# Turning the second item's queries by DMA behind a hold on the loads, with a reordered start, in a sorted-attention and maxout kernel

## The chip, the cores and the metric

The kernel runs on one core of a Trainium2 chip. The metric is the device time of one execution in microseconds. Thirteen executions of the kernel before gave a median of 167.15 us (166.62 to 169.05). A profile is one further execution taken apart by the hardware profiler; all times in it count from the start of its span.

The engines are TensorE (PE; the loading of its weights is listed as PEld), VectorE (DVE), ScalarE (ACT), GpSimd (POOL) and SyncE (SP). SP only issues DMAs here; GpSimd issues the loads[...].

## What is computed

Four items (batch entries) with 8 heads of 768 tokens and head dimension 64. The tokens of a head form 8 blocks of 96. A small matrix per head, made nearly doubly stochastic by five rounds of normalisation, mixes the blocks of keys and values ("sorts" them); attention then runs within each block, and a maxout layer with an output product follows on the 3072 tokens.

```python
for _ in range(5):
    P = P - np.max(P, axis=-1, keepdims=True)
    P = np.exp(P)
    P = P / (np.sum(P, axis=-1, keepdims=True) + 1e-09)
    P = P / (np.sum(P, axis=-2, keepdims=True) + 1e-09)
k_sorted = np.einsum('bhij,bhjcd->bhicd', P, k_b).reshape(B, H, S, D)
v_sorted = np.einsum('bhij,bhjcd->bhicd', P, v_b).reshape(B, H, S, D)
...
scores = scale * np.matmul(q_b, k_sb.transpose(0, 1, 2, 4, 3))
attn = softmax(scores)
out = np.matmul(attn, v_sb).reshape(B, H, S, D)
...
h1 = x @ w1
h2 = x @ w2
g = np.maximum(h1, h2)
return (g @ w_out).astype(np.float32)
```

Inputs and output are float32; the kernel computes in bf16 with float32 accumulation.

## The kernel before

The whole program is one unrolled list of steps, written by hand; every engine runs its share in that order. A pool `psum` of four tiles of 128 x 1024 float32 serves every product: a step that wants a tile waits until an earlier user has been read out. `evac` reads a tile out on ScalarE ("A") or VectorE ("D"); where the list doesn't say which, `pick` takes the one with the smaller account in `load`.

*Start.* The five normalisation rounds (`sinkhorn`, L271 to L290) are a chain of short VectorE instructions with one exponential per round on ScalarE. Meanwhile TensorE multiplies zeros: 86 matmuls of 142 columns at L764, and 3072 columns each in the fourth and fifth round, with zero weights (`late`) that are written when the round begins. VectorE also makes masks in the first three rounds (`masks`) and, in the third, the selections of item 0 (`selections(0, nc.vector)`). `turn_v` reorders item 0's values for the sort, mostly on ScalarE. `block_diagonals_first` turns the mixing matrix into the two operands of item 0's sorts.

*Front.* The string `front` at L779 is item 0 up to its maxout layer: `k` sorts a third of the keys, `v` a quarter of the values, `tq` turns half of the queries on TensorE, `SC` is a score step (products and one exponential), `VA` a value step (products, a reciprocal and a multiplication), `tx` transposes attention outputs, `tw` transposes one weight matrix, `h..a` and `h..b` are the two halves of a maxout product, `diff` subtracts the weight matrices on VectorE, `pe` makes the sort operands of items 1 to 3, and `F` puts 512 columns of zeros before the next score, value or maxout step. The first key sort has 1024 columns of zeros ahead of it.

*Tails.* From then on there is a list of units for each item: 8 maxout products (none left for item 0), for item 0 four products of the two output weights (`w_product`), and 12 output parts (`moe_out`; two of them fill half a tile, four are read out together). The dictionaries `first_tail`, `second_tail` and `third_tail` hang steps of the following items behind the unit of that number: `KS` (key sorts), `VS` (value sorts), `TQ` (query transposes), `SC`, `VA`, `TR` (attention outputs turned by DMA, issued by SP), `TURN` (a quarter of the value reordering, on VectorE). The value sort `sort_v_pair` handles items 1 and 2 together and needs all four turns; turns 1 and 2 read the first half of each item's values, turns 3 and 4 the second half.

*Queries.* `q_transposes` (L424) turns the queries so that head dimensions lie on partitions. Items 0 and 1 go through TensorE: 48 matmuls of 128 columns each item, and two evictions. Items 2 and 3 go through `pair_q` (two VectorE copies into `q_pair`) and two DMA transposes issued by SP.

*Loads.* All loads stand on GpSimd's queue, in the order of the program: values, keys and queries of item 0, the weights (w1 and w2 in quarters and a half, then the output weights), keys of item 1, queries of item 1, the values of items 1 and 2 in two pieces each, keys of item 2, queries of item 2 (into the space of w2), values of item 3 in four pieces (into the space of items 1 and 2, once these are turned), keys and queries of item 3. An issue that needs a buffer not yet free waits, and everything behind it on GpSimd waits too. GpSimd also writes the selections for the later items, `one_j`, and two weight differences.

## Time and profile before

| | us |
|---|---|
| median of 13 executions | 167.15 |
| the profiled execution | 166.62 |
| its span | 164.8 |
| TensorE busy | 159.4 |
| VectorE, ScalarE, GpSimd busy | 76.6, 83.0, 32.2 |
| first key sort starts | 12.14 |
| item 1's key sort starts | 37.98 |
| first value sort of items 1 and 2 starts | 50.83 |
| item 1's first maxout product starts | 70.59 |
| item 2's queries: first transpose issued, last landed | 73.00, 80.18 |
| item 3's last piece of values landed | 62.17 |

The groups of the page show the shape of the work: TensorE spends most of its time on two kinds of matmul.

```profile
L715 PE MATMUL out_ps<-wo_sb,g 128*128 128x512 bf16 (+2 forms) x200 | 48.3, 371 | 0.1
L688 PE MATMUL h_ps<-xT,w_sb 128*128 128x384 bf16 x256 | 44.5, 326 | 0.0
```

A row names the line, engine, operation and tiles, then the count; behind the first bar stand busy time in us and the mean length of one in ns, behind the second the idle time of the engine just before them. Matmuls overlap, so the mean length is not the distance between two of them: a matmul of 512 columns starts about 0.22 us after the one before it.

The page's sliced rows divide the span into 40 parts of 4.12 us; a digit is the busy share in tenths. The chain of waits is followed back from the last instruction to whatever released each step, and says what the end of the kernel hangs on. Timelines of one engine give start and length of each group of instructions.

### The profile page before, as it was taken

How to read it: one execution, taken by the hardware profiler on the slowest of the kernel's cores; microseconds unless marked ns; L12 is line 12 of the kernel's file. 1: busy time of each engine (PE TensorE's matmuls, PEld its weight loads, DVE VectorE, ACT ScalarE, POOL GpSimd, SP SyncE). 2: the span in 40 equal slices, each digit the busy share in tenths (PEclk: the TensorE clock that was granted, in tenths of full speed). 3: DMA queues.
4: the chain of work that ended last, by engine and by line, in shares of the span. 5: the costliest groups of instructions: out<-in, count | busy, mean ns of one | idle time of the engine just before them, and what ended most of it. 6: DMA issues, size and time to landing. Idle time of an engine off the chain costs nothing.

```text
span 164.8 us, 4562 instructions
## 1 busy us (share of the span) xinstructions
PE 159.4 (97%) x2018; PEld 96.1 (58%) x2018; DVE 76.6 (46%) x173; ACT 83.0 (50%) x102; POOL 32.2 (20%) x55
## 2 busy tenths in 40 slices
PE   7999899999999999999999999999999999999992
PEld 7948678656555555557555554575655546654451
DVE  5879789465474564625356973250642320000011
ACT  3585985927149846065653163557447206642020
POOL 7998396240113000000005020000000000000000
PEclk9999999999999999999999999999999999999999
DMA  3999999999999995689304999993025294000333
GB/s 46 205 204 198 198 207 206 211 203 223 211 201 211 216 241 95 183 107 241 68 0 77 154 218 199 265 224 21 0 52 175 50 164 142 0 0 0 127 131 127
DMA packets 30404, 23.90 MB, mean 145 GB/s; under 512 B 16752, under 2 KB 25200, under 8 KB 30384
## 3 DMA queue, kind: packets, MB, share of 16 engines
q0 software_dynamic: 11040, 13.37, 47.9%
q1 hardware_dynamic: 19200, 10.17, 27.5%
q8 instruction: 16, 0.26, 0.6%
q10 hardware_dynamic: 144, 0.07, 0.1%
q14 instruction: 4, 0.03, 0.1%
HBM read 26.75 MB, written 6.29 MB: 200 GB/s over the span
## 4 chain that ended last, share of the span: by engine, by line
PE 83%; DVE 9%; issue 3%; ACT 2%; DMA 1%; ACTq 0%
PE out_ps L715 34%; PE h_ps L688 26%; PE o_ps L586 4%; PE wc_ps L668 4%; PE s_ps L559 4%; PE k_ps L469 3%; PE tq_ps L444 2%; ACT e L567 2%; DVE v_dc L257 1%; PE v_ps L534 1%; PE tw_ps L649 1%; PE v_ps L490 1%; DMA p_sb<-in_sort_net_dram 1%; PE tx_ps L624 1%; DVE colsum L283 1%
## 5 line engine op out<-in xcount | busy, mean ns | idle before, releaser
L715 PE MATMUL out_ps<-wo_sb,g 128*128 128x512 bf16 (+2 forms) x200 | 48.3, 371 | 0.1
L688 PE MATMUL h_ps<-xT,w_sb 128*128 128x384 bf16 x256 | 44.5, 326 | 0.0
L688 PEld LDWEIGHTS <-w_sb 128*128 128x128 bf16 x256 | 24.0, 98 | 15.6
L567 ACT ACTIVATE e<-s_ps 96x768 bf16<-96x768 f32 x32 | 23.8, 805 | 13.5 <-PE s_ps L559 13.3
L702 ACT ACTIVATE g<-h_ps 128x768 bf16<-128x768 f32 x27 | 21.8, 810 | 17.5 <-PE h_ps L688 17.4
L715 PEld LDWEIGHTS <-g 128*128 128x128 bf16 x200 | 17.1, 97 | 15.8
L715 PE MATMUL out_ps<-wc,xT 128*128 128x512 bf16 (+2 forms) x100 | 24.8, 370 | 0.0
L108 ACT COPY o<-out_ps 128x1024 f32<-128x1024 f32 x10 | 10.1, 1012 | 28.3 <-PE out_ps L715 25.6
L603 DVE TENSOR_TENSOR x<-o_ps,rs 96x512 bf16<-96x512 f32 x32 | 22.0, 686 | 1.1
L715 PEld LDWEIGHTS <-xT 128*128 128x128 bf16 x100 | 9.6, 97 | 11.2
L586 PEld LDWEIGHTS <-e 96*128 96x128 bf16 x256 | 11.8, 97 | 5.9 <-DVE v_sb L110 0.2
L597 DVE RECIPROCAL rs<-o_ps 96x8 f32<-96x8 f32 x32 | 6.4, 201 | 17.8 <-PE o_ps L586 17.7
L750 DVE COPY o<-out_ps 128x512 f32<-128x512 f32 (+1 forms) x2 | 1.2, 625 | 27.6 <-PE out_ps L715 27.6
L586 PE MATMUL o_ps<-v_sb,e 96*128 96x65 bf16 x256 | 12.9, 193 | 0.0
L110 DVE CAST kT<-k_ps 128x1024 bf16<-128x1024 f32 x7 | 8.3, 1216 | 7.4 <-PE k_ps L469 7.4
L108 ACT CAST v_sb<-v_ps 96x1024 bf16<-96x1024 f32 x10 | 9.8, 1015 | 2.5 <-PE v_ps L490 0.9
L704 DVE TENSOR_SCALAR g<-h_ps 128x768 bf16<-128x768 f32 x5 | 4.8, 956 | 11.6 <-PE h_ps L688 11.6
L160 POOL DMA_DIRECT2D v_raw<-in_k_dram x3 | 2.5, 820 | 36.2 <-DVE rs L597 36.0
L110 DVE CAST v_sb<-v_ps 96x1024 bf16<-96x1024 f32 x6 | 7.3, 1216 | 4.5 <-PE v_ps L534 2.2
L559 PEld LDWEIGHTS <-kT 64*128 64x128 bf16 x256 | 6.1, 94 | 5.3 <-issue 3.0
L559 PE MATMUL s_ps<-qT,kT 64*128 64x96 bf16 x256 | 8.6, 204 | 0.5 <-DVE qT L110 0.3
L169 POOL DMA_DIRECT2D v_raw<-in_v_dram x11 | 5.9, 542 | 13.3 <-DVE v_dc L257 8.1
(96 smaller groups left out, 145.0 us busy)
## 6 DMA issues: line engine op xcount, KB each, us to landing
out_dram<-o SPq DMA_DIRECT2D x11, 512.0 KB, 3.1
v_raw<-in_v_dram POOLq DMA_DIRECT2D x8, 384.0 KB, 12.8
k_raw<-in_k_dram POOLq DMA_DIRECT2D x9, 256.0 KB, 9.9
w_sb<-in_moe_w_dram POOLq DMA_DIRECT2D x4, 256.0 KB, 8.4
w_sb<-in_moe_w_dram POOLq DMA_DIRECT2D x2, 512.0 KB, 11.2
wo_sb<-in_moe_w_out_dram POOLq DMA_DIRECT2D x2, 512.0 KB, 14.5
v_raw<-in_v_dram POOLq DMA_DIRECT2D x3, 256.0 KB, 5.0
q_raw<-in_q_dram POOLq DMA_DIRECT2D x4, 192.0 KB, 8.9
```

Source lines behind the costliest of these rows:

```text
L108: nc.scalar.copy(out=out_ap, in_=in_ap)
L110: nc.vector.tensor_copy(out=out_ap, in_=in_ap)
L169: nc.gpsimd.dma_start(out=v_raw[r0 : r0 + 64, m * n : (m + 1) * n], in_=v_src[b, :, m * n : (m + 1) * n],)
L559: nc.tensor.matmul(ps[:, h2 * 512 + ii * 128 : h2 * 512 + ii * 128 + BLK], kT[b][rows, (hp * 8 + i) * BLK : (hp * 8 + i) * BLK + 128], rhs ...
L567: nc.scalar.activation(out=e[:, 0 : 8 * BLK].rearrange("p (t c r) -> p t c r", t=8, r=R), in_=ps[0:BLK] .rearrange("p (t f) -> p t f", t=8 ...
L586: nc.tensor.matmul(ps[:, h2 * 512 + ii * 65 : h2 * 512 + (ii + 1) * 65], e[:, (h2 * 4 + ii) * BLK : (h2 * 4 + ii) * BLK + 128], v_sb[:, m0 ...
L597: nc.vector.reciprocal(out=rs, in_=ov[:, :, :, 64])
L603: nc.vector.tensor_tensor(out=x, in0=ov[:, :, :, 0:D], in1=rs.to_broadcast([BLK, 2, 4, D]), op=ALU.mult,)
L668: nc.tensor.matmul(ps[:, 0:512], w2T[:, fb, dmt * 128 : (dmt + 1) * 128], wo_sb[:, fb, :], start=(fb == 0), stop=(fb == NFB - 1),)
L688: nc.tensor.matmul(h_ps[ch, t][:, m * 512 : m * 512 + TCH], w1_sb[:, hp, fb * 128 : (fb + 1) * 128], xT[:, b % 2, ch, hp % 2, hp // 2, :], ...
L702: nc.scalar.activation(out=g, in_=src, func=AF.Relu)
L715: nc.tensor.matmul(dst, g_tiles[b, ch, m // 2][:, m % 2, off : off + 128] if m < NFB else xT[:, b % 2, ch, hp % 2, hp // 2, off : off + 12 ...
```

## The change

**Start.** The zero matmuls become 86 of 126 columns. The zeros ahead of the first key sort become 640 columns in matmuls of 320. `selections(0)` and the two copies that fill `maskJ` move from VectorE to GpSimd; `one_j` is zeroed as 32-bit words; on GpSimd the selections of items 1 to 3 move behind the first four weight loads, and all weight loads move behind the mask copies. The tiles of the masks are made earlier in the program.

**Front.** The string has another order, other engines for some evictions and a fourth `F`.

**Item 1's queries.** They now go the way of items 2 and 3: two copies by `pair_q` and two DMA transposes at the end of the front; the 48 matmuls and the two evictions `TQ` are gone.

**Hold.** `hold_loads(b)` is a small GpSimd copy of a few of the turned queries into a tile `seen`: it reads parts of both halves of `qT[b]`, so GpSimd passes it only when both transposes have landed. It is called for items 1 and 2.

**Loads.** Item 1's queries are loaded before its keys. Before the first hold only these and item 1's first piece of values are issued. Behind it come item 2's first piece of values, the second pieces of items 1 and 2, item 2's keys and queries. The values of item 3 move from unit 11 of the first tail to behind the second hold, at unit 0 of the second.

**Tails.** The key sort of item 1 moves behind the first weight product; its score steps stand closer together and earlier; the turns of values stand two to four units later, the value sorts three units, the value steps one to three units. In the second tail the turns of item 3's values, its value sorts, two value steps and the packing of its queries move by one or two units.

```diff
+    seen = const.tile([128, 2, 2], BF16, tag="seen", name="seen")
+
+    def hold_loads(b):
+
+        nc.gpsimd.tensor_copy(out=seen, in_=qT[b][:, 1:3, R - 1, 126:128])
...
-        if b > 1:
+        if b > 0:
...
-        keep_streaming(ps, n)
+        keep_streaming(ps, n, most=320)
...
-    keep_streaming(ps_f32("fill_ps"), 86 * 142, most=142)
+    keep_streaming(ps_f32("fill_ps"), 86 * 126, most=126)
...
-            selections(0, nc.vector)
...
+    for c, n, m in [(2, 2, 0), (4, 3, 1)]:
+        nc.gpsimd.tensor_copy(
+            out=maskJ[:, c : c + n],
+            in_=maskJ[:, m].to_broadcast([128, NB, n]).transpose([0, 2, 1]),
+        )
+    for t in range(2):
+        load_w_columns(w2_sb, moe_w2, t, t + 1)
+        load_w_columns(w1_sb, moe_w1, t, t + 1)
+    for b in range(1, B):
+        selections(b)
...
-        k0D k1A k2D v1D v2A v3A tq0D v0A tq1D SC1 SC0 F1
-        SC2 VA1 SC5 VA0 SC3 F2 VA2 SC4 F0 tx0D SC6 VA3
-        SC7 h00a VA4 tx1A tw0D h01a VA5 h01bA diff2 h00bA VA7 tx2A
-        tw1A h02a VA6 h02bA h11a diff3 tx3A h12a h03a h12bD h10a h10bA
-        pe2 h11bD h03bA h13a h13bA
+        k0A k1A k2D v0D v3A v1A tq0D v2A tq1D SC1 SC0 F3
+        VA1 SC3 F0 VA0 SC2 F2 VA3 SC4 F1 tx0D VA2 SC6
+        SC5 tw0D tx1A h00a h01a VA6 h00bA VA4 diff3 h01bA VA5 SC7
+        diff2 tw1A h03a VA7 h03bD h02a tx2D h02bA tx3D h13a pe2 h10a
+        h13bD h10bD h12a h11a h12bA h11bA
...
     load_q(1)
-    for piece in range(2):
-        for b in (1, 2):
-            load_v(b, which=piece)
-    load_k(2)
+    load_k(1)
+    load_v(1, which=0)
 
     for step in front[-26:]:
         front_step(step)
+    load.update(A=600.0, D=300.0)
+    for half in range(2):
+        pair_q(1, half)
+    for half in range(2):
+        q_transposes(1, half)
+    hold_loads(1)
+    for b, piece in [(2, 0), (1, 1), (2, 1)]:
+        load_v(b, which=piece)
+    load_k(2)
     load_q(2)
...
     first_tail = {
-        7: KS,
-        9: [TQ[0], TURN[0]],
-        10: [SC[0], TQ[1], TURN[1]],
-        11: SC[1:4] + TURN[2:4] + [lambda half=half: load_v(3, half=half) for half in range(2)],
-        12: VS[0:3],
-        13: VS[3:6],
-        14: VS[6:8] + [SC[4]],
...
+        8: KS,
+        11: SC[0:3],
+        12: SC[3:6],
+        13: SC[6:8] + TURN[0:2],
+        14: TURN[2:4],
+        15: VS[0:3],
+        16: VS[3:6],
+        17: VS[6:8],
+        18: [VA[0]],
+        19: [VA[1], TR[0]],
...
     second_tail = {
-        0: [lambda: q_transposes(2, 0), lambda: q_transposes(2, 1)],
+        0: [
+            lambda: q_transposes(2, 0),
+            lambda: q_transposes(2, 1),
+            lambda: hold_loads(2),
+            lambda: load_v(3, half=0),
+            lambda: load_v(3, half=1),
+        ],
         2: KS,
         4: SC[0:2],
         5: [VA[0]],
         6: SC[2:4],
         7: [VA[1], TR[0]],
-        8: [VA[2], TURN[0]],
-        9: [VA[3], TR[1], TURN[1]],
-        10: SC[4:7],
+        8: [VA[2]],
+        9: [VA[3], TR[1], TURN[0]],
+        10: SC[4:7] + [TURN[1]],
         11: [VA[4], TURN[2]],
```

## The prediction

> **What bounds the kernel now.** I read the page's busy table first, then its sliced rows, then the chain of waits in order of time, and last the timelines of SP and VectorE around the steps that move.
>
> ```profile
> PE 159.4 (97%) x2018; PEld 96.1 (58%) x2018; DVE 76.6 (46%) x173; ACT 83.0 (50%) x102; POOL 32.2 (20%) x55
> ...
> DMA  3999999999999995689304999993025294000333
> ```
>
> TensorE is busy 97% of the span and no other engine over 50%. A busy TensorE need not be doing useful work, so I also looked at the starts of its matmuls: between 38 us and the end only three lie over 0.2 us later than their columns explain (0.22 at 49.2, 0.24 at 51.3, 0.41 at 95.8). So after the start-up the time is the sum of TensorE's work: a matmul taken away is gained whole, and any new wait is lost whole. The DMA row is the second limit: full from slice 2 to slice 15, that is until about 62 us.
>
> ```profile
> 7.74 0.24 DVE sel_v L204 x2
> ...
> 13.14 0.42 DVE maskJ L824
> ...
> 43.24 0.79 PE tq_ps L444 x24
> ...
> 46.15 0.79 PE tq_ps L444 x24
> ```
>
> These are four pieces of the chain of waits, start and length in us. The first two are VectorE work that the start waits for; the last two are the second item's query transposes on TensorE. All four go.
>
> ```profile
> 73.00 4.69 SPq L430 DMA_TRANSPOSE qT<-q_pair  x2
> ...
> 47.85 2.31 DVE L257 COPY v_dc<-v_raw 128x768 uint32<-128x768 uint32 x3
> ```
>
> From the timelines of SP and of VectorE: how long the third item's queries take SP to issue as DMA transposes, and three of the four turns of values before the value sorts (about 0.8 us each).
>
> **What the Trainium skill says.** "DMA: Bandwidth & Descriptors", section on queues, rings and completion order: each DMA engine goes round the queues that have work, a packet at a time. So a transpose beside loads shares the engines with them. The trace agrees: the value transpose issued at 88.64 beside the last key load landed after 5.8 us, the one at 86.21 alone after 2.8 us. "TensorE: Matmul & The Clock Gate", section on the warm-up: the clock falls only after an idle window of about 3.4 us. The gap that the shorter zero matmuls leave is about 0.5 us, so I charge nothing; no row of this trace shows such a gap.
>
> **The change part by part.**
>
> *Start.* The chain loses the two selections (0.24 us); TensorE's fill before the first key sort goes from 1024 to 640 columns (at 2.4 columns per ns 0.16 us). The key sort, at 12.14 in the trace, then starts at about 11.75. The two mask copies (0.42 us) leave VectorE and the first key eviction goes to ScalarE, which frees the third key and first value evictions sooner: following the evictions by their durations (1.01 us on ScalarE, 1.2 on VectorE) I get the first value product at 18.65 instead of 19.32, 0.67 us sooner. The zero matmuls of 126 columns end before the late zeros are ready, so nothing waits for them. On GpSimd the moved memset, selections and mask copies are some 2 us of short instructions around the first weight loads; those loads stand behind earlier ones in a full DMA queue (the first lands at 17.74 us, 1.3 us after the last query), so neither end moves.
>
> *Front order.* The same steps in another order and one more fill of 512 columns (0.21 us plus a switch, about 0.24). I followed buffers and evictions by hand and found no new wait over 0.2 us. The front ends at about 37.55 instead of 37.98: **-0.43 us** with the start.
>
> *Query transposes.* 48 matmuls less, 2 x 0.79 = **-1.6 us** (a bound of 1.8 if the changes of shape around them go too). Their VectorE evictions (0.96 each) are replaced by two packings (0.55 each), which end near 38.0 us, behind the last front evictions.
>
> *When the second item's queries land.* By landings in the trace, the last of the output weights lands at 31.93; q of item 1 (4.57 us in the trace) now comes next, about 36.5; then its keys in steps of 1.25 (37.8, 39.0, 40.3), then one piece of values, 42.1. The key sort now stands behind one weight product (1.83 us) and needs its last piece at about 40.5, a margin of 0.2 us that could cost up to 0.8 if the transposes slow that piece. SP issues the transposes at 38.0. In the trace the pair took 7.2 us from first issue to last landing (73.00 to 80.18, with an output store ahead of it); its packets alone ran 3.6 us. I take first packets at 39.2, sharing with the values until 41, and the landing of the second half at 45. TensorE wants it at 47.4 (37.55 + 4 weight products of 1.83 + key sort 1.7 + two score steps), so the scores don't wait.
>
> *The hold.* GpSimd now waits for these transposes with a small copy. Behind it on GpSimd's queue stand three value pieces (item 2's first, item 1's second, item 2's second), item 2's keys and queries. The trace shows no such wait. Issue at about 45.4; first landing 3.6 us later (between 2.5 us, a step in mid-stream, and 4.4, the first load of the kernel), then 1.82 us each (item 3's values landed at 56.71, 58.51, 60.43, 62.17): the last at 52.6. The first two turns need only the first pieces and run before. The last two need 52.6 and end at 54.3. TensorE reaches the value sort at 54.35: 47.4, then four output parts of 1.35, six score steps (1.2) and 0.4 where the sixth score step waits for a buffer from the third exponential. So the likeliest new wait is 0.3 us; a landing x later than 52.6 costs x. Two more places of this stretch cost: that 0.4, and about 0.45 where the next output part waits for ScalarE's eviction (1.01 us) behind a value sort of 0.57. The 0.46 of waits at 49.2 and 51.3 goes. Sum: 0.3 + 0.85 - 0.46 = **+0.7 us** (range 0.3 to 3).
>
> *The second hold.* Item 3's values, in the trace landed at 62, are now issued when item 2's queries have landed (80.18 on the old clock). From the same figures the third piece lands near 88 and the fourth near 90. The first two turns now stand after the fourth value product, whose VectorE work ended at 88.57, and need the third piece; the last two stand 2 us later. A margin of half a microsecond; VectorE has over 1 us of slack there before TensorE runs out of buffers, so I take nothing (bound: 1.5 us lost, or the old 0.41 gained). Item 3's keys and queries follow their old places by about 1 us and are wanted 9 us later.
>
> Sum: -0.43 - 1.6 + 0.7 = -1.3 us. The profiled execution took 166.62 us, 164.8 of it the span; it would become 165.3. The median of the runs shown is 167.15, so 165.8.
>
> **The rivals.**
>
> *The loads come too late (slower).* Place: the value sort of items 1 and 2. If the transposes slow down beside keys and values (as the one at 88.64 did) and the pair's packets take 5 us, as item 3's did from 107.9 to 112.9, the second half lands at 47.5, the held pieces at 55, the turns end at 56.7 and the sort waits 2.4 us instead of 0.3; VectorE's sort evictions, queued behind the turns, add about 0.8. Sum +2.9 - 1.3 = +1.6 us, 168.8. It decides from a landing of the last piece at 54.0; measurably slower from 54.5. For it: nothing in the trace shows this wait, and my margins are tenths. Against it: the queue is empty behind the values, and the transposes issued at 76.14 with the pipe nearly free landed in 4.0 us.
>
> *Gain eaten.* The held pieces at 53.5, the keys' last piece 0.4 late: -1.3 + 0.9 + 0.4 = 0, about 167.1. For it: several waits of this size. Against: each would have to come out at its unlucky side.
>
> *All hidden.* The turned queries land at 44, the pieces at 51.6, no wait at the sort and none at 95.8: -1.3 - 0.3 - 0.4 = -2.0, 165.1. For it: TensorE is the only bound.
>
> **How the numbers follow.** About 0.3% (0.5 us) is what a measurement of this kernel can tell from no change. Likeliest case (165.2 to 166.6) 0.45; all hidden 0.17; gain eaten 0.15; too late 0.23. Faster: 0.62. Same: 0.14, most of the eaten case. Slower: 0.24, the late case and the edge of the eaten one. The range reaches from 164.7 to 168.5: below it lie savings that no row supports, above it the worse half of the late case. The likeliest case alone would give 164.9 to 166.6.
>
> **What would show it.** Right: TensorE has 47 matmuls less; the first key sort near 11.75, the second item's key sort near 39.4, in one piece; the query transposes' second landing near 45; GpSimd idle there, ended by that DMA; turns three and four end before 54.5, and the value sort starts within 0.5 us of them. Wrong: a wait of TensorE over 1 us before the value sort, in the key sort (keys slowed by transposes), or in the front (an order that runs out of buffers); a cold clock after the first zeros, seen as key-sort matmuls farther apart; or turns of the last item that wait over 2 us for values.

## The result, and the profile after

The changed kernel took 170.32 us (median of 11 executions, 168.45 to 172.47) against 167.31 us (median of 48) for the kernel before. The ratio is 1.0133, 95% interval [1.0107, 1.0160]: 1.3% slower, where 165.8 us and faster had been predicted, and outside the predicted range of 164.7 to 168.5. The ratio is smaller than that of the two medians (1.018) because it leaves out executions more than 1.5% above the fastest of their kernel, among them four of the changed kernel, three of which ran with a lowered granted clock. The first profiled execution of the changed kernel (172.04 us) was one of the longest, so the lines below come from a second one (170.05 us, span 168.2, granted clock 1.00 throughout).

From the page of that execution, the lines that answer to those shown of before: the busy time of TensorE and its weight loads, and the sliced rows of TensorE and of the DMA engines.

```profile
PE 156.8 (93%) x1952; PEld 94.5 (56%) x1971; DVE 77.2 (46%) x172; ACT 81.4 (48%) x99; POOL 32.2 (19%) x61
...
PE   7999699999999599999899989989999999999991
...
DMA  3999999999789992979399999989025253000333
```

The weight loads count 1971, as many as the 2018 matmuls of before less 47; 19 records of the matmuls themselves are missing here. So the work did go away, but TensorE is now busy for 93% of its span and not for 97%. Its row has dips that before had not, or less: deeper in slice 5 (16.8 to 21.0 us; a 6, before an 8), new in slice 14 (54.7 to 58.9) and smaller in slices 20, 24 and 27. The DMA row, which before was full until slice 15, has a hole at slices 11 and 12, between 42 and 50 us.

How far the stages had got, in us of each profile; "step's own share" is what the stage that ends there adds to the difference:

| stage starts | before | changed | difference | step's own share |
|---|---|---|---|---|
| first key sort | 12.14 | 12.00 | -0.14 | -0.14 |
| first value step of item 0 | 19.32 | 18.85 | -0.47 | -0.33 |
| end of the front | 37.98 | 38.49 | +0.51 | +0.98 |
| first output part | 49.44 | 47.99 | -1.45 | -1.96 |
| item 1's first maxout product | 70.59 | 71.69 | +1.10 | +2.55 |
| item 2's first maxout product | 104.02 | 105.88 | +1.86 | +0.76 |
| item 3's first maxout product | 135.67 | 138.72 | +3.05 | +1.19 |
| end of the span | 164.84 | 168.25 | +3.41 | +0.36 |

(The end of the front is the start of item 1's key sort, less the 1.83 us of the weight product that now stands ahead of it.) Two things have to be kept in mind. The profile of before is the shortest of the 48 executions (166.62 us), so the 3.4 us at the end are more than the 3.0 between the medians. And one score step of eight matmuls, about 0.2 us, stood ahead of the first output part in before and stands behind it now: of the 1.96 us gained there about 1.8 are saved, and of the 2.55 us lost in the next stage about 2.35 are new.

So the transposes are saved in full. It is all given back, in the front, then between the first output part and item 1's maxout layer, then in item 3. In the first profile of the changed kernel the same stages read +0.53 for the front, -1.97, +2.63, and then +0.46 and +3.69: the loss behind the first output part is steady, that in item 3 is not.

The chain of waits of the same execution (start, length) names what the last two of these stages hang on:

```profile
38.62 2.83 SPq L424
41.51 3.81 DMA qT<-q_pair
45.46 0.49 issue
45.95 0.45 POOL v_raw L169
46.46 0.51 POOL v_raw L169
46.96 7.99 DMA v_raw<-in_v_dram
55.07 1.57 DVE v_dc L250 x2
56.69 0.88 PE v_ps L528 x48
...
98.23 13.38 DMA v_raw<-in_q_dram
111.63 1.03 DVE q_pair L412 x2
112.66 1.14 DVE kT L110
113.84 2.77 PE h_ps L682 x16
```

In before the chain between 38 us and the end ran almost wholly over TensorE. Now it has left TensorE before 38 us, goes over the packing on VectorE to the query transposes at 38.62, through the hold into the held loads, and comes back only at the value sort, at 56.69. The turns of values that took 2.31 us in one row of before are split by a wait; VectorE's timeline (the bracket gives the idle time before the instruction and what ended it):

```profile
50.54 1.57 DVE L250 COPY v_dc<-v_raw 128x768 uint32<-128x768 uint32 x2 [5.95 <-DMA v_raw<-in_v_dram]
55.07 1.55 DVE L250 COPY v_dc<-v_raw 128x768 uint32<-128x768 uint32 x2 [2.96 <-DMA v_raw<-in_v_dram]
```

And TensorE's timeline shows what that costs; the first line is the same value sort in before, which waited for nothing, the other two are the changed kernel:

```profile
50.83 1.13 PE L534 MATMUL v_ps<-bd,v_dc 64*128 64x64 bf16 x48
...
53.95 1.03 PE L709 MATMUL out_ps<-wc,xT 128*128 128x512 bf16 x4
56.69 0.88 PE L528 MATMUL v_ps<-bd,v_dc 64*128 64x64 bf16 x48 [1.71 <-DVE v_dc L250]
```

The value sort starts 1.9 us later than the matmuls ahead of it need, 1.71 of it shown as idle. Why the pieces are late is seen in the busy times by stretch. A line has the stretch and its length, busy time and count of TensorE, its weight loads, VectorE, ScalarE and GpSimd, then the granted clock of TensorE (1.00 is full), the mean share of the DMA engines, which passes 1 where packets overlap, and the GB/s that they moved. Ahead of them stands the row of before's page, GB/s in 40 slices; 42 to 50 us are its eleventh to thirteenth:

```profile
GB/s 46 205 204 198 198 207 206 211 203 223 211 201 211 216 241 95 183 107 241 68 0 77 154 218 199 265 224 21 0 52 175 50 164 142 0 0 0 127 131 127
...
42.00:43.50 1.50, 1.45 (x9) 0.67 (x9) 0.28 (x1) 1.49 (x2) 0.00 (x0) 1.00 1.13 252
43.50:45.00 1.50, 1.50 (x9) 0.67 (x8) 0.69 (x1) 0.00 (x0) 0.00 (x0) 1.00 0.94 181
45.00:46.50 1.50, 1.50 (x8) 0.67 (x7) 0.00 (x0) 0.59 (x1) 0.74 (x3) 1.00 0.00 0
46.50:48.00 1.50, 1.44 (x29) 0.84 (x28) 0.00 (x0) 0.65 (x2) 1.50 (x3) 1.00 0.65 70
48.00:50.00 2.00, 1.84 (x21) 0.88 (x22) 0.00 (x0) 2.00 (x4) 2.00 (x4) 1.00 0.97 194
```

The hold stops the loads while the transposes run, and then the engines move nothing for 1.5 us and little for another 1.5: the second transpose lands at 45.32, the copy runs at 45.44, the first load is issued at 45.95, and its first packet is moved at 47.17. At 190 GB/s those 3 us are more than one value piece of 384 KB, in a stretch in which before moved some 200 GB/s without a break.

### The profile page after: what moved, and what is told of

Read it like the earlier page. It is cut to its first block, busy times and chain, and to the rows that moved or that the text cites. A ratio compares the mean times of both kernels' runs of the same rounds, so it can differ in the third digit from the quotient of the medians.

```text
span 170.2 us, 4478 instructions
## 1 busy us (share of the span) xinstructions
PE 158.2 (93%) x1971; PEld 94.3 (55%) x1971; DVE 77.5 (46%) x172; ACT 81.2 (48%) x99; POOL 32.3 (19%) x61
## 4 chain that ended last, share of the span: by engine, by line
PE 52%; DMA 27%; DVE 9%; issue 5%; POOL 2%; SPq 1%; ACT 1%; POOLq 0%; DVEq 0%
PE out_ps L709 24%; PE h_ps L682 15%; DMA v_raw<-in_v_dram 10%; DMA v_raw<-in_q_dram 9%; DMA qT<-q_pair 5%; PE o_ps L580 3%; PE s_ps L553 2%; DMA xT<-x 2%; SPq L424 1%; PE v_ps L528 1%; PE v_ps L484 1%; PE tw_ps L643 1%; POOL v_raw L169 1%; DVE q_pair L412 1%; DVE g L698 1%
## 5 line engine op out<-in xcount | busy, mean ns | idle before, releaser
L696 ACT ACTIVATE g<-h_ps 128x768 bf16<-128x768 f32 x26 | 21.0, 810 | 23.9 <-PE h_ps L682 23.8
L580 PEld LDWEIGHTS <-e 96*128 96x128 bf16 x256 | 11.6, 98 | 6.4 <-ACT e L561 0.7
L250 DVE COPY v_dc<-v_raw 128x768 uint32<-128x768 uint32 (+1 forms) x9 | 7.0, 801 | 10.7 <-DMA v_raw<-in_v_dram 10.7
L108 ACT CAST v_sb<-v_ps 96x1024 bf16<-96x1024 f32 x9 | 8.9, 1008 | 5.5 <-PE v_ps L528 2.7
L110 DVE CAST kT<-k_ps 128x1024 bf16<-128x1024 f32 x6 | 7.2, 1220 | 6.5 <-PE k_ps L463 6.5
L698 DVE TENSOR_SCALAR g<-h_ps 128x768 bf16<-128x768 f32 x6 | 5.6, 953 | 8.7 <-PE h_ps L682 8.7
L110 DVE CAST v_sb<-v_ps 96x1024 bf16<-96x1024 f32 x7 | 8.4, 1216 | 2.2 <-PE v_ps L528 1.8
```

The source lines that it names most:

```text
L108: nc.scalar.copy(out=out_ap, in_=in_ap)
L110: nc.vector.tensor_copy(out=out_ap, in_=in_ap)
L250: nc.vector.tensor_copy(out=dst.bitcast(U32).rearrange("p (d c) -> p d c", c=BLK)[:, :, c0:c1], in_=src.bitcast(U32).rearrange("p (c d) -> ...
L580: nc.tensor.matmul(ps[:, h2 * 512 + ii * 65 : h2 * 512 + (ii + 1) * 65], e[:, (h2 * 4 + ii) * BLK : (h2 * 4 + ii) * BLK + 128], v_sb[:, m0 ...
L696: nc.scalar.activation(out=g, in_=src, func=AF.Relu)
L698: nc.vector.tensor_scalar(out=g, in0=src, scalar1=0.0, scalar2=None, op0=ALU.max)
```

## The experiments

### The changed kernel once more, and its two halves

> The changed kernel once more, unaltered, for a second profile. Theory (second hold): TensorE waits 1 to 4 us in item 3's key sort, because the packing of item 3's queries stands on VectorE ahead of the key evictions and its load lands after 110 us; and about 1.5 us before the value sort of items 1 and 2. Rival (a bad draw): the profile shown was one of the longest executions, and in a typical one the wait at item 3 is under 0.5 us; the loss is then spread over the front and the first hold. Time 168.5 to 170.5 either way.

It took 170.44 us (4 executions), ratio 1.0187 [1.0146, 1.0228]; its profile is the one above.

**Start and front alone** (`e_start`): all edits of the start and the front, with item 1's queries, loads and tails as before.

> The start and the front of the change alone (126 columns, shorter fill, masks and selections on GpSimd, the new front order), with item 1's queries on TensorE and loads and tails as in the kernel before. Theory (as forecast): 0.4 us less than the kernel before, 166.8. Rival (the front gains nothing): the new order waits where the old one didn't, VectorE ending the front later; within 0.2 us of the kernel before or slower.

Measured 167.31 us (17 executions), before beside it 167.21: 1.0010 [0.9988, 1.0032]. The first value step comes at 18.85, 0.47 us sooner, as in the changed kernel, and yet the front ends at 38.58 where before ended at 37.98. In time the start and front are worth nothing, the rival's case.

**The query part alone** (`e_q1`): the changed kernel with the start and front of before.

```diff
-    keep_streaming(ps_f32("fill_ps"), 86 * 126, most=126)
+    keep_streaming(ps_f32("fill_ps"), 86 * 142, most=142)
...
-        k0A k1A k2D v0D v3A v1A tq0D v2A tq1D SC1 SC0 F3
+        k0D k1A k2D v1D v2A v3A tq0D v0A tq1D SC1 SC0 F1
```

> The second half of the change alone: the start and the front are those of the kernel before, item 1's queries, the holds, the loads and the tails those of the changed kernel. Theory (the start and front are worth nothing, the whole loss lies in the late loads behind the holds): the gap near 19.5 us is 0.4 in place of 1.1, the front ends near 38.0, TensorE waits 1.5 to 2.3 us before the value sort and 0.5 to 3.5 us behind item 3's key sort; 169.0 to 170.3, a ratio to before of 1.010 to 1.018. Rival (start and queries act on each other, since in the changed start the weights are issued later): 168.3 or less.

Measured 170.41 us (6 executions), 1.0173 [1.0134, 1.0213]: the whole loss. The front ends at 38.12, the gap near 19.5 us is 0.65 (that of before is 0.42, so not quite gone), TensorE waits 2.77 us before the value sort and 0.36 behind item 3's key sort. The second wait is smaller than expected and the first larger; the sum is what the theory had, and the two parts don't act on each other.

### The gap in the front

TensorE's timeline of the changed kernel shows the gap that grew:

```profile
19.21 0.34 PE L553 MATMUL s_ps<-qT,kT 64*128 64x96 bf16 x8
20.52 0.39 PE L82 MATMUL o_ps<-fill 128*128 128x512 bf16 x1 [0.96 <-PE s_ps L553]
```

and that of before a shorter one at the same count of instructions:

```profile
19.99 0.34 PE L559 MATMUL s_ps<-qT,kT 64*128 64x96 bf16 x8 [0.25 <-PE o_ps L586]
```

A matmul of zeros, which needs no data, starts about 1.1 us late (0.42 in before, 1.12 in `e_start`; all counted from where the matmul ahead lets it start, so the idle time shown is a little less). The bracket names only TensorE's own step ahead of it, and the chain of waits calls it "issue": no semaphore explains it. What ends it is a DMA of 16 KB on the queue that the page lists as "instruction": in the trace it begins at 18.09, and the gap ends 2.43 us later; in before it begins at 17.60 and the gap ends 2.38 later. Two kernels test this.

`e_start43`: `e_start` with the same zeros in half as many matmuls, so that everything behind them stands 86 instructions earlier in TensorE's stream.

```diff
-    keep_streaming(ps_f32("fill_ps"), 86 * 126, most=126)
+    keep_streaming(ps_f32("fill_ps"), 43 * 252, most=252)
```

> The start of the change alone, with its first zeros as 43 matmuls of 252 columns instead of 86 of 126: the same columns, 86 instructions less on TensorE ahead of everything else. Theory (TensorE waits for its instructions): the gap of 0.5 to 1.1 us near 19.4 us, behind the third score step, which no semaphore explains and which stands at the same instruction count in the kernel before, goes or moves to a later step; the front ends 0.5 to 1 us sooner than in the kernel with the start alone, time 166.3 to 166.9. Rival (a wait on data): the gap stays behind the third score step and the time is 167.3.

Measured 172.05 us (6 executions), 1.0196 [1.0146, 1.0245]. The gap at 19.4 is gone and another of 2.3 us lies at 16.0, in the middle of the query transposes of item 0:

```profile
18.39 0.85 PE L438 MATMUL tq_ps<-ident,q_raw 128*64 128x128 bf16 x12 [2.17 <-issue]
```

Its instruction transfer begins at 16.12, and the gap ends 2.27 us later. So the cause was right and the forecast wrong: the gap moved to an earlier step, not a later one, and doubled. The count explains it. If TensorE's matmuls and weight loads are numbered in order of time, the gap stands ahead of number 704 or 705 in every other kernel with a gap there, whatever that instruction is, and ahead of 448 here: 256 earlier, which would be one transfer of 16 KB at 64 bytes an instruction (an estimate from these counts). The gap follows the count of instructions, not the work.

`e_gate`: the changed kernel with the weight loads held on GpSimd until item 0's first turned queries have been read out.

```diff
     for step in front[:-26]:
         front_step(step)
+        if step == "v2A":
+            nc.gpsimd.tensor_copy(out=seen, in_=qT[0][:, 0:2, R - 1, 126:128])
+            weight_loads()
```

> The changed kernel with all weight loads held on GpSimd until item 0's first half of turned queries has been read out (about 17.4 us), so that the DMA engines have no load to move from about 16.5 to 19.5 us. It is slower as a whole, since the weights come 2 to 3 us later; only the gap of TensorE at 19.3 to 20.4 us is the question. Theory (TensorE waits for its own next instructions, whose transfer begins near 17.7 and is held up by full DMA engines): with the engines empty the gap falls under 0.5 us. Rival (the transfer takes that long by itself, or the gap has another cause): the gap stays at 1.0 us or more, wherever it then lies.

175.54 us as a whole (2 executions), 1.0459 [1.0380, 1.0539], since a weight transpose now waits 2.2 us for its weights at 25.35 and TensorE then runs at half its clock until 32.5. The question was the gap. Busy times by stretch, with the DMA share and GB/s last, and TensorE's timeline:

```profile
17.00:18.00 1.00, 1.00 (x40) 0.86 (x34) 0.60 (x2) 0.94 (x2) 0.59 (x2) 1.00 0.00 0
18.00:19.00 1.00, 0.59 (x13) 0.26 (x8) 0.65 (x1) 1.00 (x2) 1.00 (x2) 1.00 0.00 0
```

```profile
19.18 0.34 PE L553 MATMUL s_ps<-qT,kT 64*128 64x96 bf16 x8
19.46 0.39 PE L82 MATMUL o_ps<-fill 128*128 128x512 bf16 x1
```

With the DMA engines running empty (from about 15 us on) the instruction transfer begins at 15.29 in place of 18.09, and the same matmul follows the scores at once. So TensorE ran out of instructions, and it did so because their transfer stood in line with loads that keep the DMA engines full.

All other profiles agree: in each the first instruction behind the gap starts 2.3 to 2.5 us after the transfer began. The length of the gap varies from one execution to the next, from 0.3 to 1.2 us with the new start (eleven profiles) and from 0.4 to 0.9 with that of before (four), so 1.1 against 0.42 is in part the draw. TensorE comes to this point about 0.2 us sooner with the new start and leaves it, in both, when the instructions are there, at 20.0 to 20.5 us: what the start had gained by then is lost.

### The holds

**Without the first** (`e_nohold1`), the line `hold_loads(1)` taken out:

> Only the first hold is gone; the second stays. Theory (the transposes need the hold): item 1's queries share the DMA engines with the loads and land after 48 us, TensorE waits 1 to 4 us at item 1's first scores; the wait at the value sort (1.8 us in the profile) goes; time 168 to 171. Rival (the hold only costs): the transposes land before 47 all the same, and the time falls by 1.5 to 2 us against the changed kernel.

180.76 us (4 executions), 1.0829 [1.0782, 1.0877]. TensorE's timeline at item 1's first scores:

```profile
58.23 0.82 PE L553 MATMUL s_ps<-qT,kT 64*128 64x96 bf16 x16 [10.91 <-DMA qT<-q_pair]
```

Beside the loads the two transposes took until 58.1 and 59.5 us where they land by 45.3 with the hold. The theory was right in kind and far too mild (a wait of 1 to 4 us, 168 to 171 us). The hold isn't optional. "DMA: Bandwidth & Descriptors" of the Trainium skill, in its section on queues, rings and completion order, says that an engine goes round its queues by packets. The trace agrees that the transposes share the engines with the loads, and come off badly. In its records the packets of the transposes carry 256 bytes each and those of the loads 768 (queries), 2048 (keys) and 6144 (values); that this is why the shares are so uneven is likely but not shown.

**Without the second** (`e_nohold2`), item 3's values loaded at unit 14 of the first tail:

```diff
-        14: TURN[2:4],
+        14: TURN[2:4] + [lambda half=half: load_v(3, half=half) for half in range(2)],
...
-            lambda: hold_loads(2),
-            lambda: load_v(3, half=0),
-            lambda: load_v(3, half=1),
```

> The second hold is gone: item 3's values are issued right behind the last turn of items 1 and 2, as in the kernel before. Theory (second hold): item 3's queries land near 106 us, the wait in item 3's key sort goes, and the time is 1.5 to 2.5 us below the changed kernel, 167 to 168. Rival (crowding): the values now land between 65 and 73 us beside the attention outputs and queries that SP turns, these come late, TensorE waits at item 2's first maxout products or scores, and the time stays within 0.5 us of the changed kernel.

172.55 us (4 executions), 1.0318 [1.0268, 1.0367]. Here it is item 1's attention outputs, also turned by DMA, that are starved:

```profile
74.95 2.40 PE L682 MATMUL h_ps<-xT,w_sb 128*128 128x384 bf16 x7 [2.96 <-DMA xT<-x]
```

In before those loads had landed by 62.2 us, and the first attention output was issued at 60.5. The first hold has pushed them to 67.6 to 73.2 us, into the outputs, and the second hold is what keeps them out. The rival was right about the crowding; that it costs 2 us more than the second hold was not expected by either.

**The second alone** (`e_hold2`): the kernel before with `hold_loads(2)`, item 3's values behind it, and the changed second tail.

> The kernel before, with the second hold alone: item 3's values are issued when item 2's queries have landed, and the second tail is that of the changed kernel. Theory (the second hold costs by itself): item 3's queries land 4 us or more later than in the kernel before, their packing blocks VectorE ahead of item 3's key evictions, TensorE waits 0.5 to 3 us there; time 168 to 170. Rival (the second hold is harmless and only the first one's delay makes it late): no wait over 0.3 us in item 3's key sort, time 167.0 to 167.5.

167.72 us (20 executions), 1.0016 [0.9995, 1.0036]. Item 3's queries land at 107.95 (105.25 before) and TensorE doesn't wait for them. The second hold alone is harmless, as the rival had it: its delay fits into the slack.

**Fewer loads behind the first hold.** `e_early` puts one more of the three held value pieces ahead of it, `e_both` two (and loads item 3's queries elsewhere, see below).

```diff
     load_v(1, which=0)
+    load_v(2, which=0)
...
-    for b, piece in [(2, 0), (1, 1), (2, 1)]:
+    for b, piece in [(1, 1), (2, 1)]:
```

> The changed kernel, with item 2's first piece of values issued before the first hold instead of behind it. Theory (the wait before the value sort is the time of three held loads after the hold): the transposes of item 1's queries land 1 to 2 us later, at 45.5 to 47, still before the scores want them; the last piece lands about 1.5 us sooner and the wait before the value sort falls from 1.9 to 0.3 to 1 us; time about 1 us below the changed kernel. Rival (transposes starve beside any load): they land after 48, TensorE waits over 1 us at the scores, and nothing is gained or it gets slower.

168.88 us (18 executions), 1.0069 [1.0046, 1.0093]. The transposes land at 45.44 and 46.69, later than in the changed kernel (43.71 and 45.32); the last piece at 54.18 (54.95), and the wait before the value sort is 1.06 us (1.87). TensorE doesn't wait at the scores; the theory held.

> The changed kernel with two edits: three of the four value pieces of items 1 and 2 stand ahead of the first hold (one in the changed kernel), and item 3's queries are loaded as in e_q3. Theory (both holds only put loads too late): the turned queries of item 1 land near 46.5 and 48, the one held piece is issued near 48.5 and lands near 52.5, the wait before the value sort (1.8 us) falls under 0.4; item 3's wait is gone; 166.5 to 167.5, that is no slower than the kernel before and perhaps faster. Rival (what the transposes lose by more loads ahead of them is as much): item 1's first scores wait 1 us or more for the turned queries, and the time stays over 168.5.

168.42 us (6 executions), 1.0034 [0.9996, 1.0073]. TensorE's timeline:

```profile
47.61 0.52 PE L551 MATMUL s_ps<-qT,kT 64*128 64x96 bf16 x16 [0.31 <-DMA qT<-q_pair]
48.80 0.34 PE L551 MATMUL s_ps<-qT,kT 64*128 64x96 bf16 x8 [0.68 <-DMA qT<-q_pair]
...
56.21 0.88 PE L526 MATMUL v_ps<-bd,v_dc 64*128 64x64 bf16 x48 [0.50 <-DVE v_dc L248]
```

Before the value sort only 0.5 us of idle time are left, but now the scores wait 1.0 us for the queries, which land at 47.48 and 48.76. The rival was right about the mechanism, and missed the time by little (over 168.5). With these loads and this order of steps, what is put ahead of the hold delays the queries and what is put behind it delays the values.

### Item 3

In the changed kernel item 3's queries are issued at 98.23 and land at 111.61; VectorE packs them (`pair_q`) ahead of item 3's key evictions, so TensorE, which needs a buffer back, waits 1.0 us at 112.7. In the first profile they landed at 113.61 and the wait was 3.6 us.

**Values of item 3 by pieces** (`e_pieces`), the first pieces of both halves ahead of the second ones:

```diff
-            lambda: load_v(3, half=0),
-            lambda: load_v(3, half=1),
+            lambda: [load_v(3, which=p, half=h) for p in range(2) for h in range(2)],
```

> The changed kernel, with item 3's values issued first half of both row halves first, so that the first two turns can run one load earlier and item 3's keys are issued earlier. Theory (crowding behind the second hold): keys are issued 1.5 to 3 us sooner, item 3's queries land sooner by about as much, and the wait in item 3's key sort shrinks by 0.5 to 1.5 us; time 168.5 to 169.8. Rival (the queries wait for their space, which the fourth turn sets, not for keys): landing and wait as in the changed kernel, time within 0.5 us of it.

171.50 us (4 executions, 169.19 to 175.78), 1.0157 [1.0091, 1.0223], too wide a spread to see a gain of this size. In the profile a lowered clock (last section) makes everything before item 3 some 1.3 us later, so its times are counted from the issue of item 3's values. The keys are issued 9.2 us behind it (10.6 in the changed kernel), so they do go out sooner, as the theory had it. The queries are issued 14.7 us behind it (15.6) but land 28.7 us behind it (29.0), and the wait is 0.8 us (1.0): hardly any of it arrives.

**Packing behind the key sort** (`e_pair3`):

```diff
-        19: [lambda: pair_q(3, 0), lambda: pair_q(3, 1)],
...
-        0: [lambda: q_transposes(3, 0), lambda: q_transposes(3, 1)],
-        2: KS,
+        2: KS
+        + [lambda: pair_q(3, 0), lambda: pair_q(3, 1)]
+        + [lambda: q_transposes(3, 0), lambda: q_transposes(3, 1)],
```

> The changed kernel with item 3's packing and query transposes moved behind item 3's key sorts in the program, so that the key evictions no longer stand behind the packing on VectorE. Theory: the wait behind the key sort goes, but the queries land no sooner (111 to 114) and their transposes at 117 to 121, and item 3's first scores, which come up near 116, wait for them instead: the wait only moves, and the time stays within 1 us of the changed kernel's 170.4. Rival (only the order on VectorE costs): no new wait at the scores, 168 to 169.4.

172.94 us (4 executions), 1.0318 [1.0261, 1.0375]: the wait moved, as expected, and is larger than in the profile above, which was not. TensorE's timeline:

```profile
114.67 2.44 PE L682 MATMUL h_ps<-xT,w_sb 128*128 128x384 bf16 x14 [1.32 <-DMA xT<-x]
119.36 0.52 PE L553 MATMUL s_ps<-qT,kT 64*128 64x96 bf16 x16 [2.25 <-DMA qT<-q_pair]
```

The scores wait 2.25 us for the turned queries, and the maxout products wait for an attention output whose DMA was issued at 102.78 and landed at 114.63. Not only the queries are late there: so is an output that is in flight with them. In sum this is no more than the 3.6 us of the first profile, so part of it may be the draw.

**Queries of item 3 into item 2's place** (`e_q3`). They were loaded into the second half of the values' space and so had to wait for all turns of values; item 2's queries are packed long before, so their place is free.

```diff
-        if b == 2:
+        if b >= 2:
             t = w2_sb.rearrange("p t f -> p (t f)")[:, 0 : H * R * D].rearrange(
...
             lambda: load_v(3, half=1),
+            lambda: load_q(3),
...
-        12: [VA[5], TR[2], TURN[3], lambda: load_k(3), lambda: load_q(3)],
+        12: [VA[5], TR[2], TURN[3], lambda: load_k(3)],
```

> The changed kernel with one edit: item 3's queries are loaded into item 2's old place (the space of w2) right behind item 3's values, not into the space of the values behind item 3's keys. Theory (in the changed kernel TensorE waits 1.0 to 3.6 us before the maxout products behind item 3's key sort because these queries land at 111 to 114 us, VectorE's packing waits for them and the key evictions stand behind the packing): the queries land near 100, the packing waits for nothing, that wait of TensorE falls under 0.2 us, item 3's maxout starts 1 to 3 us sooner (136.5 to 137.5 in place of 138.7) and the time falls by 1 to 2.5 us, to 168 to 169.3. Rival (the DMA's crowd, not the place in the queue): the queries now run beside item 2's turned attention outputs between 94 and 100; item 2's first maxout product, 105.9 in the changed kernel, comes 1 us or more later and the time stays at 170.

169.23 us (4 executions), 1.0101 [1.0038, 1.0163]. The queries land at 99.54; the key evictions (first line, VectorE) wait for nothing but the key sort, and the maxout products (second line, TensorE) run through in one piece of 24:

```profile
110.69 2.36 DVE L110 CAST kT<-k_ps 128x1024 bf16<-128x1024 f32 x2 [7.00 <-PE k_ps L461]
...
111.59 4.07 PE L680 MATMUL h_ps<-xT,w_sb 128*128 128x384 bf16 x24
```

Item 2's maxout starts at 105.96 (105.88 in the changed kernel), so the rival's price isn't paid, although one attention output issued at 90.35 landed only at 104.58. Item 3's maxout starts 1.1 us sooner. The theory held; the gain in time isn't clear of the noise by itself.

### The mended version

`e_best` joins `e_early` and `e_q3`; `e_best_b` is the same with the start and front of before.

> The changed kernel with two value pieces of the four ahead of the first hold (as e_early) and item 3's queries loaded into item 2's old place behind item 3's values (as e_q3). Theory (the two waits are separate and their savings add: about 0.8 us at the value sort, 1 us in item 3): wait at the value sort near 1.0, none at item 1's first scores, none in item 3; 167.6 to 168.4. Rival (what one saves the other takes back): 168.8 or more.

> The same as e_best with the start and the front of the kernel before. Theory (the front of the change brings a gap of 1.1 us for its instructions where the kernel before has 0.4): 166.9 to 167.6, no slower than before. Rival (the gap is not what separates them): the same as e_best within 0.3 us.

`e_best`: 168.26 us (6 executions), 1.0065 [1.0046, 1.0084]; `e_best_b`: 168.25 us (6), 1.0061 [1.0040, 1.0082]. The front makes no difference, so the rival of `e_best_b` was right. In both the wait before the value sort is larger than expected (1.80 and 1.37 us in the profiles, against 1.06 in `e_early`); item 3's key sort and maxout wait for nothing. The time of `e_best` lies where its theory had it, but by the ratio, which is taken against executions of before beside it, it is no faster than `e_early` (1.0069): that the two savings add is not shown. No version with item 1's queries turned by DMA beat the kernel before; the interval of the nearest, `e_both`, reaches from equal to 0.7% slower.

## Why the prediction was wrong

**The bound: right.** TensorE's work is the time: what was saved on it is visible in full at the first output part, and the waits that follow are lost whole.

**Start and front, "-0.43 us": wrong.** The start's own steps were partly right (first key sort 12.00, predicted 11.75; first value step 18.85, predicted 18.65). The step that failed is "I followed buffers and evictions by hand and found no new wait over 0.2 us". That covered data and buffers, and the wait is for instructions: 0.42 us in before, 1.1 in the changed kernel. The gap of before was there to be seen, and the prediction had looked for odd gaps only from 38 us on. In the two profiles the term is +0.5, all of it from the end of the gap (20.5 against 20.0 us); in time, by `e_start`, nothing.

**Query transposes, "-1.6 us": right**, at the larger end: about 1.8, the bound that was named, of the 1.96 from the front's end to the first output part.

**When the queries land, "45": right** (45.32, and 44.85 in the first profile). The key sort didn't wait, but by luck: its last keys landed at 40.80, not 40.3, and the sort came to them about 0.9 us later than predicted, because the front ended late.

**The hold, "0.3": the mechanism was right and the size was wrong**, and this is the largest error. The prediction said "Issue at about 45.4; first landing 3.6 us later", "then 1.82 us each", "the last at 52.6". Measured: issue 45.95 (+0.55), first landing 4.47 us later (+0.87), the two others 4.53 us after it and not 3.64 (+0.89): 54.95. The failed step is that landing: it was set between a step in a running stream and a cold start, and after a hold it is a cold start. The bound named for it, 4.4 us, is what was measured, and in every profile with the first hold it is 4.4 to 5.5 us. The later pieces were priced at the step of a running stream; why two of them took 0.89 more wasn't looked into. The turns end at 56.64, TensorE had come to the value sort at about 54.8, and so it waits 1.9 us and not 0.3.

The sums on TensorE's side hold a slip. Four weight products, the key sort and two score steps at 0.2 us each make 47.0 and not 47.4, and a sort reached at 54.35 behind turns that end at 54.3 would not wait for 0.3 us. With 47.0 TensorE is at the sort at about 53.9; that it came there 0.9 us later is the late front, and without it the wait would have been longer still.

Of the other waits of that stage, the 0.4 at the sixth score step came (0.37). The 0.45 at an output part didn't: at 60.1 us a matmul starts 0.32 us late in this profile, but about 0.2 of it is a matmul whose record is missing, and the first profile, which has all records, shows 0.10 there. And of the 0.46 that was to go, the 0.22 ahead of the first output part is still there. So the term, forecast at +0.7, is about +2.35, of which 2.2 are the waits at the value sort and the sixth score step.

**The second hold, "nothing": right for the values, wrong for what stands behind them.** Item 3's third and fourth pieces landed at 92.0 and 93.9, not at 88 and 90, still without a wait at the sort. The step that failed is "Item 3's keys and queries follow their old places by about 1 us and are wanted 9 us later". The queries were issued 2.6 us later than before and landed 6.4 us later, with attention outputs in flight beside their 768 KB; and they were wanted sooner than the scores, by the packing that stands ahead of the key evictions on VectorE. Cost 1.0 us here, 3.6 in the first profile. `e_hold2` shows that the second hold alone doesn't bring this wait, `e_q3` that the landing is its cause; what slows the landing was not taken apart.

**Not in the prediction:** about 0.6 us at 80 us, where item 2's scores wait for its turned queries (landed 81.58, before 80.18). `e_start` has a wait of 0.55 there too, so not all of it comes from the hold. The old 0.41 at 96 us, which the prediction left as it was, is gone, and 0.50 at 100 us, where an output part waits for an eviction, has taken its place. And 0.36 us lies behind the landing of the last store. It appears in every kernel with item 1's queries turned by DMA that was looked at (29.5 us from item 3's maxout to the end, against 29.2 in `e_start` and `e_hold2`); its cause was not looked into.

**The rivals.** "The loads come too late" has the right place, the value sort, and figures that look like a hit: pieces at 55 (54.95), turns ending at 56.7 (56.64), a wait of 2.4 us (1.9). But it came to them by another road. It let the transposes crawl beside keys and values, so that the second half lands at 47.5; that half landed at 45.32, and the time was lost behind the landing, in the restart of the loads. That the figures agree is luck. Its time of 168.8 is still short of 170.3, because it let the start keep its gain and item 3 its slack. It was given 0.23: the margins were seen to be tenths of a microsecond, but each was set at its middle.

## What to carry to other kernels

A wait that holds back loads empties the DMA engines: price the restart as a cold start, issue and first packets included (here some 3 us at little or no traffic), and move on with that delay through every later transfer, asking of each who wants it first, which may be a copy that stands ahead of more urgent work on its engine. Where loads fill the DMA as here, a step turned into a DMA transpose may need such a hold, so the two prices belong in one sum: here 1.8 us saved on TensorE against 1.9 us of waiting at the value sort alone. And look at the gaps of the bounding engine from the start of the span on, above all at those that no semaphore explains.

## What was not expected of the hardware

**TensorE can wait for its own instructions.** They come in DMAs of 16 KB, some 6 us apart in the first 30 us (11.6, 17.6 and 23.6 in before). Beside full DMA engines the one near 18 us left TensorE idle for 0.3 to 1.2 us (2.3 in `e_start43`, near 16 us), ending 2.3 to 2.5 us after the transfer began. Without traffic (`e_gate`) there was no such gap.

**The granted clock can fall after a short gap.** Busy times by stretch, as above. First `e_start43` in and after its gap of 2.3 us, then `e_pieces` after its gap of 1.2:

```profile
16.00:18.40 2.40, 0.23 (x10) 0.07 (x5) 0.37 (x1) 0.97 (x2) 1.64 (x3) 0.73 1.45 197
18.40:20.00 1.60, 1.60 (x28) 1.43 (x28) 0.71 (x1) 0.00 (x0) 0.68 (x1) 0.50 1.46 197
22.00:24.00 2.00, 1.96 (x28) 1.08 (x25) 0.97 (x3) 1.50 (x2) 2.00 (x2) 0.51 1.25 208
```

```profile
20.40:22.00 1.60, 1.47 (x21) 0.88 (x22) 0.76 (x2) 0.43 (x1) 1.07 (x2) 0.76 1.27 207
22.00:24.00 2.00, 2.00 (x28) 1.49 (x27) 1.29 (x4) 1.18 (x2) 2.00 (x2) 0.50 1.23 205
```

In `e_start43` the clock is at half from 17.12 to 23.95 us, so it falls 1.1 us after the gap began; in `e_pieces` from 21.22 to 24.63, 0.7 us after the gap ended. Item 1's key sort in `e_pieces` is 1.4 us later than in the changed kernel for it (41.75 against 40.32). The length of a gap alone doesn't decide it. After nearly the same gap the second profile of the changed kernel kept a clock of 1.00, and so did longer ones elsewhere: 2.8 us before the value sort in `e_q1`, 3.6 us in item 3 in the first profile. "TensorE: Matmul & The Clock Gate" of the Trainium skill, in its part on the clock gate, gives an idle window of about 3.4 us, and the prediction charged nothing on that ground for short gaps; here the clock fell after gaps of 1.2 and 2.3 us, and what else it takes is not shown.

**DMA transposes lose to loads.** With held value pieces, keys and queries let go beside them, a pair of transposes that otherwise took 6.7 us from first issue to last landing took about 21 (`e_nohold1`); issuing the two alone kept SP busy for 16.7 us, against 4.4.
